# Block B's q and k: x tiles 2 and 3 by Strassen's algorithm, alternating with plain groups, with the loads around them at other times

## The chip, the cores and the metric

The kernel runs on one core of a Trainium2 chip. Its engines work side by side, each through a list of instructions of its own: TensorE (PE) multiplies matrices, with PEld its loads of weights; VectorE (DVE) and ScalarE (ACT) do elementwise work; GpSimd (POOL) does elementwise work too; SyncE (SP) issues the transfers, which 16 DMA engines carry out. SBUF is the memory on the chip, PSUM the eight banks that matmuls write to. The metric is the device time of one execution in microseconds, lower is better, as a median of several.

## The reference

Two attention blocks over the same shapes, S = 2048 rows, D = 640, 32 heads of 20. Both begin with x @ wqkv and end with a product by wo; the outputs are concatenated.

```python
# both blocks
q, k, v = split((x @ wqkv).reshape(1, 2048, 3, 32, 20))   # x 2048x640, wqkv 640x1920
# A: every position s looks at s, s-2, ... s-14 (W = 8, dilation 2), earlier ones masked
kg, vg = k[:, :, s - 2 * arange(8)], v[:, :, s - 2 * arange(8)]
out_A = softmax(einsum("bhsd,bhswd->bhsw", q, kg) * 20 ** -0.5) weighted over vg, then @ wo
# B: full attention
out_B = softmax(q @ k.T * 20 ** -0.5) @ v, then @ wo
```

## The kernel before, in words

Each factor of a product of x and a weight is split into a high part, rounded to a shorter format (fp32r), and the low rest; a product of 128x128 by 128x512 is then three matmuls (PASSES: high-high, high-low, low-high). x is transposed in DRAM and cut into four tiles of 512 columns for each block; D = 640 is five chunks of 128 rows, of which a tile keeps four in a buffer of the tag "big" (xn) and the fifth in "last0" or "last1" (xl). `a_split(hi, lo, raw)` makes a split: ScalarE casts the high part, VectorE subtracts for the low one.

The program runs through stages on TensorE:

- A's q and k, until 137.3 us. `a_four` computes them already by the Strassen-Winograd scheme (sums of quarters of x and of w instead of an eighth product), and `a_narrow` the remaining narrow columns. POOL makes the x sums for it (`x_sums`).
- B's q and k, 137.3 to 274.2 us, the stage that the change is about. The 1280 columns of q and k are ten groups of 128 (the order is MS), taken two at a time: for each pair, four x tiles by two groups, 40 results of 128x512 with 15 matmuls each. A result goes from its PSUM bank by a ScalarE cast (high part) and a VectorE subtraction (low part) to an SBUF tile (tags "pa" and "pb", three buffers each), and from there by one SP transfer to DRAM, as `kb_d` or `qb_d`. A weight group comes by one transfer into a "stg" buffer and is split into a "w" buffer (four of these).
- V of both blocks, from 274.2 us. Blocks 0 and 1 of the loop are four plain groups of 15 matmuls 128x128x320 each; their results (`ro`, tag "r", four buffers) are copied by ScalarE and stored to `va_d`. From block 2 the matmuls are made of 64-row halves, and between them stand the first products of B's q and k (`b_max`, which finds the maxima of the softmax), from tiles `bk` and `bq` that `b_pieces(0)` loads back from `kb_d` and `qb_d`. bk and bq take buffers of the tag "big".
- the main loop, where B's scores and values alternate on TensorE, and at the end the products by wo.

A's attention itself runs on POOL all along, in units paced by `a_pace` with constants such as QK_US; twelve units (the scores of three row tiles) stand ahead of V.

The order of instructions on each engine is fixed by the program: the wrapper `InOrder` keeps it as written, `tick()` counts steps, and `after(n, fn)` puts code n steps later. So an instruction that waits holds everything behind it on its engine. SP issues almost all transfers in one such order. The tags' numbers of buffers set when a load can start: a tile gets the buffer of the oldest one of its tag when that has been read for the last time. PSUM banks are handed out by `all_banks` in a fixed turn of eight in the stages before V; in V, a list `free` of four is used.

In the listing, all operations that go through the wrapper carry its line, L71; groups in the profile are told apart by the names of the tiles and their shapes.

Of the kernel before, what the change touches and what calls it, by code (L numbers as in the profile page):

```python
# [17 lines left out]
S = 2048  # L18
# [32 lines left out]
QK_US = 3.42  # L51
# [24 lines left out]
def attention_pair(ctx, tc, xa, wqk_a, wv_a, wo_a, xb, wqk_b, wv_b, wo_b, oa, ob):  # L76
# [498 lines left out]
    XB, WB = [], []  # L575
# [88 lines left out]
    def w_ask(n):  # L664
        w, fns = m_pieces(MS[n])
        WB.append(w)
        fns[0]()
# [20 lines left out]
    p_next[:] = "bbbaaa"  # L688
    b_load(1)
    a_narrow(2)  # L690
    b_load(2)
# [7 lines left out]
    XB.append(w)  # L699


# [33 lines left out]
    def x_raw(c):  # L735

        out = []
        for a, b in PAIRS:
            raw = p_tile()[:, :(b - a) * 512].rearrange("p (k c) -> p k c", c=512)
            sp.dma_start(raw, (xa, xb)[c // 4][a * 128:b * 128, c % 4 * 512:c % 4 * 512 + 512].rearrange("(k p) c -> p k c", p=128))  # L740
            out.append((a, b, raw))
# [4 lines left out]
    def xv_ask():  # L746

        t = columns(0)
        XV.append((t, None))
        for j, (tag, bufs) in enumerate((("vb", 2), ("aot", 1))):  # L750
            raw = sb.tile([128, 1280], F32, tag=tag, bufs=bufs, name="xr")
            for k, c0, n, r in ((2 * j, 0, 2, raw[:, :1024].rearrange("p (k c) -> p k c", c=512)), (4, 256 * j, 1, raw[:, 1024:].unsqueeze(1))):
                c = r.shape[2]
                sp.dma_start(r, xa[k * 128:(k + n) * 128, c0:c0 + c].rearrange("(k p) c -> p k c", p=128))
                u, m = t[k // (KC - 1)], k % (KC - 1)
                after(8, a_split, u[:, 0, m:m + n, c0:c0 + c], u[:, 1, m:m + n, c0:c0 + c], r)

    groups = 0
    gp.us = 0.0
    for m in range(0, 10, 2):  # L760
        nxt = []
        for n in range(4):
            for j in range(2):
                p = next(banks)
                for k in range(KC):
                    for i, (wi, xi) in enumerate(PASSES):
                        pe.matmul(p, WB[j][:, wi, k], chunk(XB[n], xi, k), start=(k == 0 and i == 0),
                                  stop=(k == KC - 1 and i == 2))
                c = MS[m + j]
                o = (0, 1) if c < KC else (1, 0)  # L770
                pt = p_pair(F32R)
                act.copy(pt[:, o[0]], p)
                dve.tensor_tensor(pt[:, o[1]], p, pt[:, o[0]].bitcast(F32), ALU.subtract)
                after(1, sp.dma_start, dst_b(c, n).rearrange("t p c -> p t c"), pt.bitcast(F32))
                tick()
                if loads:
                    loads.pop(0)()
                if m < 8 and n == (m == 0):
                    w, loads = m_pieces(MS[m + 2 + len(nxt)])
                    nxt.append(w)  # L780
                elif m == 6 and (n, j) == (2, 0):
                    xv_ask()
                elif m == 6 and (n, j) == (3, 0):
                    w0, loads = wide_pieces(wv_a[0])
                elif m == 8:
                    g8 = 2 * n + j
                    if g8 == 1:
                        k_loads, q_loads = b_pieces(0)
                    elif 1 < g8 < 6:
                        k_loads.pop(0)()  # L790
                        if g8 == 5:
                            xraw = x_raw(1)
                        if g8 == 3:
                            wait[0] = 7
                            w1, more = wide_pieces(wv_a[1])
                            for fn in more:
                                fn()
                    elif g8 == 6:
                        for _ in range(4):
                            q_loads.pop(0)()  # L800
                groups += 1
                if groups > 4:
                    a_pace(A_SLOW * QK_US * groups)
        WB = nxt
# [472 lines left out]
    def x_parts(c, raws, second=gp):  # L1277
# [6 lines left out]
        for a, b, raw in raws:  # L1284
            u, m = t[a // (KC - 1)], a % (KC - 1)
            hi, lo = (u[:, x, m:m + b - a] for x in range(2))
            act.copy(hi, raw)
            if c not in (2, 3):
                second.tensor_tensor(lo, raw, hi.bitcast(F32), ALU.subtract)

# [7 lines left out]
    for block in range(15):  # L1298
        c, half = divmod(block, 2)
        s0 = c % 4 * 4  # L1300
        if block < 2:
            for s in range(s0, s0 + 4):
                v_group(c, half, s)
                v_tick(2.2, False)
                if (block, s) == (0, 3):
                    x_parts(1, xraw, dve)
                    xraw = x_raw(2)
# [227 lines left out]
```

## Time and profile before

| | |
|---|---|
| median of 3 runs | 1720.01 us (1719.5 to 1721.14) |
| the profiled execution | 1720.44 us, of which the span on the core is 1718.4 |
| TensorE busy | 1708.8 us, 99% of the span |
| VectorE, ScalarE, POOL busy | 1458.6, 1335.6, 1316.5 us |
| B's q and k on TensorE | 137.29 to 274.21 us |
| V's blocks 0 and 1 on TensorE | 274.21 to 291.90 us |

How to read the rows: a row of a window gives the stretch, its length, then busy time and number of instructions of each engine, TensorE's granted clock (1.00 is full speed), the mean busy share of the 16 DMA engines and GB/s. A row of a group gives line, engine, operation, output tile <- input tiles, shapes and number, then busy time and mean ns of one, then the idle time ahead of it and what ended it. A row of the timeline gives start and duration in us, engine, line, operation, tiles and number of instructions run together; in brackets the idle time before it with what ended it. A row of waits gives the engine, what it waited for, then us in total, number of waits and the longest. SPq is the queue of transfers that SP issues.

### The profile page before, as it was taken

How to read it: one execution, taken by the hardware profiler on the slowest of the kernel's cores; microseconds unless marked ns; L12 is line 12 of the kernel's file. 1: busy time of each engine (PE TensorE's matmuls, PEld its weight loads, DVE VectorE, ACT ScalarE, POOL GpSimd, SP SyncE). 2: the span in 40 equal slices, each digit the busy share in tenths (PEclk: the TensorE clock that was granted, in tenths of full speed). 3: DMA queues.
4: the chain of work that ended last, by engine and by line, in shares of the span. 5: the costliest groups of instructions: out<-in, count | busy, mean ns of one | idle time of the engine just before them, and what ended most of it. 6: DMA issues, size and time to landing. Idle time of an engine off the chain costs nothing.

```text
span 1718.4 us, 34879 instructions
## 1 busy us (share of the span) xinstructions
PE 1708.8 (99%) x12627; PEld 990.3 (58%) x12627; DVE 1458.6 (85%) x1975; ACT 1335.6 (78%) x2637; POOL 1316.5 (77%) x1175
## 2 busy tenths in 40 slices
PE   9999999999999999999999999999999999999999
PEld 8888889999544544444444444444444445434459
DVE  8554334889899999999999999999999999999537
ACT  6213224232799999999999999999999999999972
POOL 4110990589999999999999999999999973486352
PEclk9999999999999999999999999999999999999999
DMA  6548979966843364345436345542644532111123
GB/s 196 183 158 265 327 259 281 304 196 207 221 138 104 102 185 132 102 128 161 129 112 168 115 124 129 171 136 84 164 135 117 140 99 75 40 49 41 34 73 118
DMA packets 207844, 253.53 MB, mean 148 GB/s; under 512 B 89788, under 2 KB 131004, under 8 KB 206680
## 3 DMA queue, kind: packets, MB, share of 16 engines
q1 hardware_dynamic: 206232, 249.67, 48.8%
q8 instruction: 99, 1.62, 0.4%
q10 hardware_dynamic: 1440, 1.64, 0.3%
q14 instruction: 73, 0.60, 0.1%
HBM read 183.70 MB, written 67.53 MB: 146 GB/s over the span
## 4 chain that ended last, share of the span: by engine, by line
PE 82%; POOL 9%; DVE 3%; ACT 2%; DMA 2%; issue 1%; SPq 0%; POOLq 0%; DVEq 0%; ACTq 0%
PE ps_st L71 82%; POOL akv L71 5%; DVE mx L71 3%; ACT stg L71 1%; POOL braw L71 1%; POOL ao L71 1%; POOL xn L71 1%; POOL ww L71 0%; DMA stg<-wqk_a 0%; DMA stg<-xa 0%; DVE wg L71 0%; POOL al L71 0%; SPq L71 0%; DMA stg<-wo_a 0%; ACT more L71 0%
## 5 line engine op out<-in xcount | busy, mean ns | idle before, releaser
L71 DVE TENSOR_REDUCE mx<-ps_st 128x1 f32<-128x512 f32 (+1 forms) x1504 | 1228.6, 876 | 56.1 <-PE ps_st L71 46.7
L71 ACT ACTIVATE stg<-ps_st 128x512 f32<-128x512 f32 x2000 | 1046.1, 630 | 41.4 <-PE ps_st L71 28.0
L71 PE MATMUL ps_st<-bk,bq 60*128 60x512 f32 x2048 | 553.7, 436 | 0.7 <-DVE mx L71 0.3
L71 PE MATMUL ps_st<-bq,bk 62*128 62x512 f32 x2048 | 549.0, 432 | 1.0 <-ACT e L71 0.9
L71 PE MATMUL ps_st<-stg,vb 128*32 128x512 f32 x4000 | 531.6, 604 | 0.4
L71 PEld LDWEIGHTS ps_st<-bq,bk 62*128 62x128 f32 x2048 | 274.9, 184 | 399.2 <-ACT stg L71 241.8
L71 POOL TENSOR_TENSOR braw<-braw,more 128x512 f32<-128x512 f32 x224 | 289.4, 1292 | 58.8 <-ACT more L71 56.6
L71 PEld LDWEIGHTS ps_st<-bk,bq 60*128 60x128 f32 x2048 | 257.1, 184 | 108.2 <-DVE mx L71 61.3
L71 POOL TENSOR_TENSOR akv<-akv 128x640 f32<-128x640 f32 (+3 forms) x304 | 284.0, 934 | 14.4
L71 POOL TENSOR_TENSOR akv<-akv,aq 128x1280 f32<-128x1280 f32 x64 | 188.2, 2941 | 76.5 <-PE ps_st L71 76.5
L71 PEld LDWEIGHTS ps_st<-stg,vb 128*32 128x32 f32 x4000 | 79.5, 108 | 143.5 <-issue 70.4
L71 POOL TENSOR_TENSOR akv<-akv,al 128x1280 f32<-128x1280 f32 x64 | 151.5, 2367 | 0.7 <-DMA akv<-va_d 0.5
L71 ACT COPY more<-ps_st 128x512 f32<-128x512 f32 x224 | 137.6, 614 | 2.7 <-PE ps_st L71 2.2
L71 ACT COPY ro<-ps_st 128x320 f32<-128x320 f32 (+2 forms) x130 | 52.6, 453 | 108.7 <-PE ps_st L71 76.9
L71 DVE TENSOR_TENSOR ro<-ps_st,ro 128x320 f32<-128x320 f32 (+1 forms) x112 | 61.9, 574 | 86.2 <-PE ps_st L71 78.2
L71 PE MATMUL ps_st<-ww,xn 64*128 64x320 f32 (+1 forms) x1392 | 123.9, 307 | 0.0
L71 PEld LDWEIGHTS ps_st<-ww,xn 64*128 64x128 f32 (+1 forms) x1392 | 117.7, 185 | 3.6 <-ACT stg L71 0.7
L71 PE MATMUL ps_st<-xn,w 128*128 128x512 f32 x480 | 115.9, 390 | 0.0
L71 PE MATMUL ps_st<-ww,aot 64*128 64x320 f32 x960 | 100.4, 309 | 1.5 <-POOL aot L71 1.5
L71 PEld LDWEIGHTS ps_st<-xn,w 128*128 128x128 f32 x480 | 90.0, 188 | 19.5 <-DVE xn L71 0.2
L71 PEld LDWEIGHTS ps_st<-ww,aot 64*128 64x128 f32 x960 | 90.4, 186 | 8.0 <-POOL aot L71 2.0
L71 ACT CAST stg<-ps_st 128x512 fp32r<-128x512 f32 x40 | 23.4, 589 | 76.1 <-PE ps_st L71 76.1
(116 smaller groups left out, 1329.4 us busy)
## 6 DMA issues: line engine op xcount, KB each, us to landing
akv<-ka_d SPq DMA_DIRECT2D x128, 320.0 KB
akv<-va_d SPq DMA_DIRECT2D x128, 320.0 KB
kb_d<-stg SPq DMA_DIRECT2D x20, 512.0 KB
qb_d<-stg SPq DMA_DIRECT2D x20, 512.0 KB
bk<-kb_d SPq DMA_DIRECT2D x16, 640.0 KB
bq<-qb_d SPq DMA_DIRECT2D x64, 160.0 KB
stg<-xb SPq DMA_DIRECT2D x16, 512.0 KB
rb<-s_d SPq DMA_DIRECT2D x128, 64.0 KB
```

The source lines that it names most:

```text
L71: return self.tc.keep_in_program_order(op(*a, **k))
```

## The change

The 600 matmuls of B's q and k become 570. x tiles 0 and 1 stay plain (`b_plain`). For each pair of weight groups, x tiles 2 and 3 become four Strassen parts (`b_four`: one, second, third, fourth, with 12, 15, 15 and 12 matmuls) which take sums of quarters of the weights (`s_sums` on VectorE, split by `s_parts` into the tiles sx) and of x (four differences on POOL in `other`, split into the tiles tx, named T1 to T4, by `t_split`, with VectorE's subtraction for T2 and T3 and POOL's for T1 and T4). Products are added from PSUM into the result tiles by VectorE (`plus`), ScalarE casts the high part (`high`), VectorE subtracts in SBUF (`done`). The list `plan` sets the order: five plain groups, then a Strassen part and a plain group in turn; the last pair's four Strassen parts follow each other.

Loads and other work move with it. x tiles 2 and 3 come raw into "akv" buffers, as do V's x tiles 0 and 1 (`xv_ask`, before in "vb" and "aot", or in the p tiles). `b_load` of x tiles 0 and 1 is at steps 17 and 20 of A's stage. The weights of V are asked for at two parts of the plan (`v_ask`), and `b_pieces(0)` is called after the last part. The memsets of four tiles with ones go from VectorE to POOL behind the stage, QK_US is 3.25 for 3.42, and the list of PSUM banks is turned by two at V's block 9.

On SP, from the last results of q and k to V's stores (qb_d<-stg is a result's store, bk and bq are loads for b_max, stg<-wv_a and stg<-xa are loads for V, va_d<-ro is a V store). Before:

```order
L71 DMA bk<-kb_d 40x4096
L71 DMA qb_d<-stg 128x2x512
L71 DMA bk<-kb_d 22x4096
L71 DMA stg<-xa 128x2x512 x2
L71 DMA stg<-xa 128x512
L71 DMA qb_d<-stg 128x2x512
L71 DMA bq<-qb_d 20x1024
L71 DMA bq<-qb_d 40x1024
L71 DMA bq<-qb_d 20x1024
L71 DMA bq<-qb_d 40x1024
L71 DMA qb_d<-stg 128x2x512
L71 DMA va_d<-ro 128x320 x4
```

After the change:

```order
L71 DMA bk<-kb_d 40x4096
L71 DMA bk<-kb_d 22x4096
L71 DMA bk<-kb_d 40x4096
L71 DMA bk<-kb_d 22x4096
L71 DMA va_d<-ro 128x320 x2
L71 DMA bq<-qb_d 20x1024
L71 DMA bq<-qb_d 40x1024
L71 DMA va_d<-ro 128x320
L71 DMA bq<-qb_d 20x1024
L71 DMA bq<-qb_d 40x1024
L71 DMA va_d<-ro 128x320
```

All four bk loads now stand in one piece behind the last q stores, and the V stores behind them.

On VectorE, at the start of B's q and k (stg<-ps_st is a result, ve a tile of ones, w a weight's low part, xn and xl those of x, sx and tx the low parts of sums; the raw halves of x tiles 2 and 3 are xr). Before:

```order
L71 TENSOR_TENSOR xn<-stg,xn 128x1024 x2
L71 TENSOR_TENSOR xl<-stg,xl 128x512
L71 MEMSET ve 128x347 x4
L71 TENSOR_TENSOR stg<-ps_st,stg 128x512 x3
L71 TENSOR_TENSOR xn<-stg,xn 128x1024
L71 TENSOR_TENSOR stg<-ps_st,stg 128x512
L71 TENSOR_TENSOR xn<-stg,xn 128x1024
```

After the change:

```order
L71 TENSOR_TENSOR xn<-xr,xn 128x1024
L71 TENSOR_TENSOR xl<-xr,xl 128x256
L71 TENSOR_TENSOR w<-stg,w 128x640
L71 TENSOR_TENSOR stg<-ps_st,stg 128x512
L71 TENSOR_TENSOR xn<-xr,xn 128x1024
L71 TENSOR_TENSOR sx<-stg,sx 128x256
L71 TENSOR_TENSOR tx<-stg,tx 128x256 x2
L71 TENSOR_TENSOR sx<-stg,sx 128x256
L71 TENSOR_TENSOR stg<-ps_st,stg 128x512
L71 TENSOR_TENSOR xl<-xr,xl 128x256 x2
L71 TENSOR_TENSOR stg<-ps_st,stg 128x512
L71 TENSOR_TENSOR w<-stg,w 128x640
```

The second pair's first weight (w) and the parts of the weights' sums (sx, and tx for two of them) now stand there, between the first results; the tiles of ones are gone from it.

The diff, cut to what the text speaks of:

```diff
 NEG = -1.0e30
 STEP = 2.36
 AHEAD = 2.4
-QK_US = 3.42
+QK_US = 3.25
 V_US = 2.72
 A_SLOW = 0.78
...
+    def w_raw(m, j):
+        WR[m, j] = sb.tile([128, KC, 128], F32, tag="stg", bufs=3, name="stg")
+        sp.dma_start(WR[m, j], wqk_b[MS[2 * m + j]])
+    def w_take(m, j):
+        w = WT[m, j] = sb.tile([128, 2, KC, 128], F32R, tag="w", bufs=4, name="w")
+        a_split(w[:, 0], w[:, 1], WR[m, j])
+    SB, TB = {}, {}
...
+    def x_pair():
+        t2, t3 = columns(2), columns(3)
+        XB[2], XB[3] = t2, t3
+        r2 = akv_raw(xb, 2)
+        after(2, other, t2, t3, r2)
+    def other(t2, t3, r2):
+        r3 = akv_raw(xb, 3)
+        (x11, x21), (x12, x22) = ((r[0][3], r[2][3]) for r in (r2, r3))
...
+        def t_split(n, raw, eng):
+            hi, lo = TB[n]
+            for k in range(2):
+                act.copy(hi[k], raw[:, k])
+                eng.tensor_tensor(lo[k], raw[:, k], hi[k].bitcast(F32), ALU.subtract)
+        for p in r2:
+            after(3, put, t2, p)
+        after(7, put, t3, r3[2])
+        for out, a, b in ((x11, x12, x11), (x12, x22, x12), (x22, x22, x11), (x21, x21, x22)):
+            after(7, pool, out, a, b, ALU.subtract)
+        after(5, w_take, 1, 0)
+        after(6, homes)
+        after(7, s_parts, 0)
+        for p in (r3[1], r3[3]):
+            after(8, put, t3, p)
+        after(9, w_take, 1, 1)
+        for n, (at, raw, eng) in {2: (9, x22, dve), 3: (9, x12, dve), 1: (10, x11, gp), 4: (10, x21, gp)}.items():
+            after(at, t_split, n, raw, eng)
+        after(8, w_raw, 1, 1)
+    def s_sums(m):
+        (a11, a12), (a21, a22) = ((WR[m, j][:, :2], WR[m, j][:, 2:4]) for j in range(2))
+        for out, a, b, op in ((a22, a21, a22, ALU.add), (a21, a11, a21, ALU.subtract), (a11, a22, a11, ALU.subtract), (a12, a12, a11, ALU.subtract)):
+            dve.tensor_tensor(out, a, b, op)
+    def s_parts(m):
+        j0, j1 = (WR.pop((m, j)) for j in range(2))
+        for n, r in (("2", j0[:, :2]), ("3", j1[:, :2]), ("1", j1[:, 2:4]), ("4", j0[:, 2:4])):
+            a_split(*(u.rearrange("p (k c) -> p k c", c=128) for u in SB[n]), r)
...
     for at, *fns in ((2, lambda: x_load(2)), (4, lambda: x_split(2, xr[2])), (5, lambda: x_sums(xr[2])), (7, lambda: s_split(2, xr[2]), constants),
                      (9, lambda: x_load(3)), (11, lambda: x_split(3, xr[3])), (12, lambda: x_sums(xr[3])), (14, lambda: s_split(3, xr[3])),
-                     (20, lambda: b_load(0))):
+                     (17, lambda: b_load(0)), (20, lambda: wait.__setitem__(0, 6), lambda: b_load(1))):
         steps_a[at] = fns
     for n in (1, 2, 3):
         for r in range(2):
             a_four(n, r, step)
         if n == 1:
             a_narrow(1)
-    wait[0] = 3
-    w_ask(0)
-    w_ask(1)
+    for j in range(2):
+        w_raw(0, j)
+        after(3, w_take, 0, j)
+    after(4, s_sums, 0)
     p_next[:] = "bbbaaa"
-    b_load(1)
+    x_pair()
+    after(4, w_raw, 1, 0)
...
-    ones = [sb.tile([128, 16 * VC + 11], F32, tag=tag, bufs=3 if tag == "raw" else 2, name="ve")
-            for tag in ("raw", "rb", "raw", "rb")]
-    for t in ones:
-        dve.memset(t, 1.0)
-    w, loads = x_pieces(xb, 3)
-    XB.append(w)
...
+        def prod(a, b, c4=None):
+            p = next(banks)
...
+        def tile_of(j, n):
+            pt = P4[j, n] = p_pair(F32R)
+            return low(j, n)
+        def low(j, n):
+            return P4[j, n][:, 1 if MS[m + j] < KC else 0].bitcast(F32)
+        def plus(p, a, out):
+            dve.tensor_tensor(out, p, a, ALU.add)
+        def high(j, n):
+            act.copy(P4[j, n][:, 0 if MS[m + j] < KC else 1], low(j, n))
+        def done(j, n):
+            pt, o = P4[j, n], MS[m + j] >= KC
+            dve.tensor_tensor(pt[:, 1 - o], low(j, n), pt[:, 0 + o].bitcast(F32), ALU.subtract)
+            b_out(MS[m + j], n, pt)
+        def one():
+            act.copy(tile_of(0, 2), prod("11", "11"))
+            p = prod("S2", "T2")
+            plus(p, low(0, 2), tile_of(0, 3))
+        def second():
+            plus(prod("12", "21", (0, 2)), low(0, 2), low(0, 2))
+            high(0, 2)
+            p = prod("S3", "T3")
+            plus(p, low(0, 3), tile_of(1, 2))
+            done(0, 2)
+        def third():
+            p = prod("S1", "T1")
+            plus(p, low(0, 3), low(0, 3))
+            plus(p, low(1, 2), tile_of(1, 3))
+            plus(prod("S4", "22", (0, 3)), low(0, 3), low(0, 3))
+            high(0, 3)
+            done(0, 3)
+        def fourth():
+            plus(prod("22", "T4", (1, 2)), low(1, 2), low(1, 2))
+            high(1, 2)
+            plus(prod(None, None, (1, 3)), low(1, 3), low(1, 3))
+            done(1, 2)
+            high(1, 3)
+            done(1, 3)
+        return [one, second, third, fourth]
...
+    plain = [(0, 0, 0), (0, 0, 1), (1, 0, 0), (0, 1, 0), (0, 1, 1)]
+    rest = iter([(m, n, j) for m in range(5) for n in range(2) for j in range(2) if (m, n, j) not in plain])
+    plan = [("p", *u) for u in plain]
+    for m in range(5):
+        for n in range(4):
+            plan.append(("q", m, n))
+            if m < 4:
+                plan += [("p", *u) for u in islice(rest, 1)]
...
+        def one(hi, lo, raw):
+            act.copy(hi, raw)
+            gp.tensor_tensor(lo, raw, hi.bitcast(F32), ALU.subtract)
+        for i, p in enumerate(akv_raw(xa, n)):
+            after(*((3 + i, put, t, p) if n else (3, put, t, p, one)))
+    def v_ask():
+        w = wide_pieces(wv_a[len(w01)])
+        w01.append(w[0])
+        for fn in w[1]:
+            fn()
+    def pieces():
+        loads_0.extend(b_pieces(0))
+        for n, fn in enumerate(loads_0[0] + loads_0[1][:4]):
+            after(n // 2 + 1 + n // 4, fn)
...
+    def at(what, fn, *args):
+        events.setdefault(what, []).append((fn, args))
+    for m in range(4):
+        at(("q", m, 0), s_sums, m + 1)
+        if m < 3:
+            at(("q", m, 0), w_raw, m + 2, 0)
+            at(("q", m, 2), w_take, m + 2, 0)
+        at(("q", m, 2), s_parts, m + 1)
+        if m < 3:
+            at(("q", m, 2), w_raw, m + 2, 1)
+            at(("q", m, 3), w_take, m + 2, 1)
+    at(("q", 3, 2), wait.__setitem__, 0, 2)
+    at(("q", 3, 2), v_ask)
+    at(("p", 4, 1, 0), xv_ask, 0)
+    at(("q", 4, 1), wait.__setitem__, 0, 3)
+    at(("q", 4, 1), v_ask)
+    at(("q", 4, 2), xv_ask, 1)
+    at(("q", 4, 3), pieces)
     gp.us = 0.0
-    for m in range(0, 10, 2):
-        nxt = []
-        for n in range(4):
-            for j in range(2):
-                p = next(banks)
-                for k in range(KC):
-                    for i, (wi, xi) in enumerate(PASSES):
...
-        WB = nxt
+    four = []
+    for n, what in enumerate(plan):
+        if what[0] == "p":
+            b_plain(*what[1:])
+        else:
+            if what[2] == 0:
+                four = b_four(what[1])
+            four[what[2]]()
+        tick()
+        for fn, args in events.pop(what, ()):
+            fn(*args)
+        if n > 5:
+            a_pace(A_SLOW * QK_US * (n + 1))
+    assert not events and next(rest, None) is None
+    (w0, w1), (k_loads, q_loads) = w01, loads_0
+    q_loads = q_loads[4:]
+    ones = [sb.tile([128, 16 * VC + 11], F32, tag=tag, bufs=3 if tag == "raw" else 2, name="ve")
+            for tag in ("raw", "rb", "raw", "rb")]
+    for t in ones:
+        gp.memset(t, 1.0)
...
     for block in range(15):
+        if block == 9:
+            free.extend([free.pop(0), free.pop(0)])
         c, half = divmod(block, 2)
         s0 = c % 4 * 4
         if block < 2:
```

More of the change, by code (lines that the diff above doesn't have):

```diff
@@ new lines, in b_plain @@
+    def b_plain(m, n, j):
+        c, W = MS[2 * m + j], WT[m, j]
+        p = next(banks)
+        for k in range(KC):
+            for i, (wi, xi) in enumerate(PASSES):
+                pe.matmul(p, W[:, wi, k], chunk(XB[n], xi, k), start=(k == 0 and i == 0), stop=(k == KC - 1 and i == 2))
+        o = (0, 1) if c < KC else (1, 0)
+        pt = p_pair(F32R)
+        act.copy(pt[:, o[0]], p)
+        dve.tensor_tensor(pt[:, o[1]], p, pt[:, o[0]].bitcast(F32), ALU.subtract)
+        b_out(c, n, pt)
```

116 lines of the change are left out of this document (57 added, 59 removed).

## The prediction

> **What bounds the kernel now.** I read the page's busy times first, then TensorE's waits, then the stretches of the program, then the groups of instructions and the queues of the stretch that changes.
>
> ```profile
> span 1718.4 us, 34879 instructions
> PE 1708.8 (99%) x12627; PEld 990.3 (58%) x12627; DVE 1458.6 (85%) x1975; ACT 1335.6 (78%) x2637; POOL 1316.5 (77%) x1175
> ```
> ```profile
> PE ps_st L71 <- POOL aot L71: 1.5, 2, 0.8
> ```
> ```profile
> 137.30:274.20 136.90, 136.90 (x602) 112.52 (x601) 51.03 (x67) 37.92 (x63) 84.11 (x80) 1.00 0.85 285
> 274.20:291.90 17.70, 17.70 (x122) 17.50 (x120) 5.71 (x7) 7.13 (x13) 0.00 (x0) 1.00 0.89 273
> ```
> TensorE is busy for 1708.8 of 1718.4 us; the largest sum in the list of its waits is 1.5 us. In block B's q and k (137.30 to 274.20) and the first two blocks of V (to 291.90) it never pauses, and its clock is 1.00 in both (the column ahead of the DMA share). So time goes only if matmuls go, and any wait that the change opens on TensorE is paid in full. In the same rows VectorE (51.03) and ScalarE (37.92) have much room in q and k; the DMA engines have little, at shares of 0.85 and 0.89.
>
> ```profile
> 137.29 2.93 PE L71 MATMUL ps_st<-xn,w 128*128 128x512 f32 x12
> ...
> 144.14 2.88 PE L71 MATMUL ps_st<-xn,w 128*128 128x512 f32 x12
> ```
> ```profile
> 274.21 1.92 PE L71 MATMUL ps_st<-ww,xn 128*128 128x320 f32 x12
> ...
> 291.90 2.10 PE L71 MATMUL ps_st<-ww,xn 64*128 64x320 f32 x23
> ```
> **Matmuls removed.** The first row is the start of q and k, the third the start of V. Forty groups of 15 are 600 matmuls in 274.21 - 137.29 = 136.92 us, 0.2282 us each. A pair of weight groups on x tiles 2 and 3 takes 12 + 15 + 15 + 12 = 54 instead of 60, all of the same size, so five pairs lose 30: -6.85 us. V would start at 267.36, and its block 2 at 291.90 - 6.85 = 285.05. A pair now holds 114 matmuls, 26.0 us.
>
> **VectorE.**
>
> ```profile
> L71 DVE TENSOR_TENSOR stg<-ps_st,stg 128x512 fp32r<-128x512 f32 x39 | 26.7, 688 | 59.1 <-ACT stg L71 59.1
> L71 ACT CAST stg<-ps_st 128x512 fp32r<-128x512 f32 x39 | 22.9, 589 | 73.3 <-PE ps_st L71 73.3
> L71 DVE TENSOR_TENSOR w<-stg,w 128x640 fp32r<-128x640 f32 x8 | 10.9, 1360 | 8.4 <-ACT w L71 8.4
> L71 DVE TENSOR_TENSOR xn<-xr,xn 128x1024 fp32r<-128x1024 f32 x2 | 2.4, 1222 | 0.3 <-ACT xn L71 0.3
> L71 DVE TENSOR_TENSOR xl<-xr,xl 128x256 fp32r<-128x256 f32 x2 | 0.8, 418 | 0.0
> L71 ACT CAST xn<-xr 128x1024 fp32r<-128x1024 f32 x2 | 2.1, 1052 | 0.0
> L71 ACT CAST xl<-xr 128x256 fp32r<-128x256 f32 x2 | 0.8, 401 | 0.0
> L71 ACT CAST w<-stg 128x640 fp32r<-128x640 f32 x8 | 5.8, 731 | 9.6 <-DMA stg<-wqk_b 9.6
> ```
> Per pair VectorE has 4 plain results and 8 sums from PSUM (12 x 0.688), 4 differences in SBUF (`done`, 128x512 again and taken at the same 0.688), 4 weight sums and 4 parts (8 x 0.418) and 2 weight splits (0.83): 8.26 + 2.75 + 3.34 + 1.66 = 16.0 us, against TensorE's 26.0. ScalarE gets one more 0.589 us cast a pair, hidden in its idle 99 of 137 us. The 14 operations that read two SBUF tiles are the doubtful ones:
>
> ```profile
> 162.34 0.83 DVE L71 TENSOR_TENSOR w<-stg,w 128x640 fp32r<-128x640 f32 x1 [1.22 <-ACT w L71]
> ...
> 234.56 2.63 DVE L71 TENSOR_TENSOR w<-stg,w 128x640 fp32r<-128x640 f32 x1
> ```
> ```profile
> 21.44 6.08 POOL L71 TENSOR_TENSOR rw<-rw 128x1024 f32<-128x1024 f32 x2 [0.69 <-DVE wc L71]
> ...
> 168.47 2.94 POOL L71 TENSOR_TENSOR akv<-akv,aq 128x1280 f32<-128x1280 f32 x1 [76.45 <-PE ps_st L71]
> ...
> 233.54 2.96 POOL L71 TENSOR_TENSOR akv<-akv,aq 128x1280 f32<-128x1280 f32 x1
> ...
> 305.62 0.74 POOL L71 TENSOR_TENSOR al<-al,am 128x256 f32<-128x256 f32 x1 [48.09 <-DVE am L71]
> ```
> ```profile
> L71 POOL TENSOR_TENSOR akv<-akv 128x640 f32<-128x640 f32 (+3 forms) x48 | 42.0, 875 | 3.8
> ```
> The weight split is 0.83 us ahead of POOL's first unit (168.47). At 234.56 it takes 2.63 and ends at 237.19, 0.69 us after POOL's multiply (233.54 + 2.96 = 236.50): it stood behind the rest of a whole POOL instruction. Of the eight in the 1360 ns row two ran ahead of POOL's start, so the other six averaged (8 x 1.360 - 2 x 0.83)/6 = 1.54, a wait of 0.71 each. At that rate 14 operations make 16.0 + 9.9 = 25.9 us a pair: just TensorE's pace. I take no loss in the steady state. [...]
>
> **The start of the stage.** The hand-written order puts this on TensorE's path. x tile 2's halves go into a buffer that A's last group frees at 137.29. ScalarE then casts two pieces of 1.05 and two of 0.40, copies two results of A (0.43 for the copy further below, which is a little larger) and casts the second pair's first weights (0.73): 4.4 us, about 141.8, and VectorE's 0.83 for the low part ends at 142.6; the third plain group needs it from 144.14 on. T2 is needed by the first pair's second product, after five plain groups and six matmuls (137.29 + 81 x 0.2282 = 155.8), and by the same rows is ready at about 153.3. So the chains have some 1.5 and 2.4 us of room if VectorE is not held up. But POOL now makes the four x sums of 128x1024 just then (two of that size took 6.08, 3.04 each), and VectorE's queue holds five operations with two SBUF inputs up to that weight split and ten more up to T2. Lower bound: they slip past, 0. Upper bound: a sum ahead of nearly every one puts the split at 147.4 (2.8 us late) and, behind it, the load and cast of the pair's other weights (its buffer is released by VectorE's parts) and T2 another 2.5: 5.3. I take the excess of the 1360 ns row over 0.83, 0.53 an operation, which is the nearest mean: four after the first make 2.1, 0.6 beyond the room; eight more make 4.2, less 2.4 and the 0.6 already paid, 1.2. Together +1.8.
>
> **The start of V.** b_pieces(0) moves behind the last Strassen part, since bk and bq take the buffers of x tiles 2 and 3. SP's order has the four bk loads after the last q stores and ahead of all V stores.
>
> ```profile
> 269.73 0.43 SPq L71 DMA_DIRECT2D bk<-kb_d  x1
> ```
> ```profile
> 437.17 1.44 SPq L71 DMA_DIRECT2D bk<-kb_d  x4
> ...
> 445.16 0.33 SPq L71 DMA_DIRECT2D stg<-wo_a  x1
> ...
> 454.79 0.80 SPq L71 DMA_DIRECT2D akv<-va_d  x2
> ```
> ```profile
> SPq L71 <- DMA bk<-kb_d: 12.9, 4, 4.4
> ```
> ```profile
> bk<-kb_d SPq DMA_DIRECT2D x16, 640.0 KB
> ```
> ```profile
> 290.72 0.43 ACT L71 COPY ro<-ps_st 128x320 f32<-128x320 f32 x1 [4.39 <-DMA va_d<-ro]
> 291.64 1.18 ACT L71 COPY ro<-ps_st 128x320 f32<-128x320 f32 x3 [0.49 <-PE ps_st L71]
> ```
> Before, the last bk went out at 269.73, 4.5 us ahead of V's start. Even so the fifth V copy stood 4.39 us for the first V store (the "r" tag has four buffers) and started at 290.72, when block 2 (291.90) needed the banks of copies five and six within 1.2 us. The same four loads issued in one go at 437.17 held SP, by 12.9 us in four waits, until 454.79: 17.6 us. In the changed order V's start is 267.36, the last q stores' differences end about 2.5 us later, and the loads go out at about 270.8; the last lands at about 288.4, the first V store behind it about 288.7, copies five and six end by 289.2 and 289.8, and TensorE waits from 285.05 to some 289.9. That is +4.9. Bounds: 0, if the loads ran at the 273 GB/s of the stretch (four of at most the 640 KB of the issue list, 9.6 us, landed by 280.4); upwards 6.6, if the last q stores or the second V store add 1.7. I take 4.9, since the row at 437.17 shows the very same four loads. bq comes behind them, at about 290 to 291; its first use is a few matmuls into block 2, which by then has just begun.
>
> **The rest, at nothing.** The memsets of `ones` and the low parts of V's first x tile, on POOL, lie in its 48.09 us wait for the softmax's maximum (up to 305.62); without it they would push A's units back by their own length (a sum of 128x1024 is 3.04). SP's x loads are four DMAs instead of three for x tiles 2 and 3 and V's tile 1, issued ahead of need while SP has idle time. A's pace (3.25 for 3.42) follows the shorter stage. The turn of the bank list at block 9 changes which bank, not when. V's weights are asked for at the parts q32 and q41, several groups of 3.4 us ahead of V's start.
>
> **Sum** on the profiled execution, 1720.44 us (1718.4 of span and 2.04 around it): -6.85 + 1.8 + 4.9 = -0.15. That execution lies 0.43 over the median 1720.01; against the median the sum is 1719.9, which I give as 1720.0.
>
> **Rivals.**
> 1. The covers hold: V stores pass the bk loads, or the loads take nearer 9.6 than 17.6 us. For it: 273 GB/s is the stretch's mean. Against: the four waits of SP on them. Then 1713.2 without early wait, 1715.0 with 1.8.
> 2. Slower: VectorE, taking turns with POOL, becomes the bound of q and k. Room is (26.0 - 16.0)/14 = 0.715 an operation, and the mean of six was 0.71. Each 0.06 more over the four pairs in which POOL works is 14 x 0.06 x 4 = 3.4 us of lag at the stage's end, which PSUM's eight banks hide from TensorE there but which makes the last q stores, hence bk and the V stores, that much later. From 0.775 on it decides: 1723.5; at 0.80 it is 14 x 0.085 x 4 = 4.8, 1724.8. The early chain's 5.3 instead of 1.8 has the same cause and alone gives 1723.5. For it: the 2.63 us at 234.56; and a unit of POOL is one multiply of 2.96 and four additions of 0.875, back to back, so that an operation which comes at any moment and stands until the running instruction ends waits on average (2.96 x 2.96/2 + 4 x 0.875 x 0.875/2)/6.46 = 0.9 us, 16.0 + 12.6 = 28.6 us a pair and 4 x 2.6 = 10.4 us of lag: 1730. Against: the measured mean of six, and POOL starts late in the first pair.
> 3. The pause lowers TensorE's clock. No row of before has a TensorE pause of this length inside the kernel, and all its clocks are 1.00, so nothing shown speaks for or against. If one V group (2.2 us, an eighth of 274.21 to 291.90) ran at half rate after the pause, that is 2.2: 1722.2. [...]
>
> That the matmuls are not saved is excluded by the order, which has 54 in a pair.
>
> **How the numbers follow.** A measurement can tell about 0.2% (3.44 us) from no change: faster is below 1716.6, slower above 1723.4. Main case, early wait 0 to 2.8 and V's start 4.9: 1718.1 to 1720.9, chance 0.42. Rival 1, 1713.2 to 1716.4: 0.28. Rival 2, 1723.5 to 1730: 0.20. Rival 3, 1720 to 1723: 0.10. Thus faster 0.28, same 0.51, slower 0.21. The range 1713.5 to 1724.5 leaves out about 0.06 of rival 1 and 0.12 of rival 2.
>
> **What would show it.** Right: V's first group at 267 to 270; TensorE idle 4 to 6 us at the start of block 2, with ScalarE's fifth copy waiting for va_d and SP waiting for bk; small TensorE waits near 144 and 156 for VectorE's w and tx; w splits of 0.8 to 2.6 us. Wrong: no pause at block 2 (rival 1); V's first group past 272 or VectorE busy without idle time in q and k (rival 2); a clock under 1.00 after the pause (rival 3).

## The result, and the profile after

The changed kernel takes 1738.4 us (median of 4 runs, 1738.0 to 1739.5) against 1720.0 of the kernel before on the same chip (median of 3 runs): a ratio of 1.0107, 95% interval 1.0087 to 1.0127. A fourth run of the kernel before took 2237.4 us and is left out. The change makes the kernel slower by some 18 us, although its q and k have 30 matmuls less. The profiled execution has a span of 1736.3 us, 17.9 more than before.

TensorE's waits, first those of the whole kernel after the change, then its timeline where they stand (start, duration, matmuls; in brackets the idle time ahead):

```profile
PE ps_st L71 <- ACT ro L71: 8.6, 1, 8.6
PE ps_st L71 <- DVE w L71: 7.2, 2, 4.2
```
```profile
136.68 2.93 PE L71 MATMUL ps_st<-xn,w 128*128 128x512 f32 x12
...
187.73 4.14 PE L71 MATMUL ps_st<-xn,w 128*128 128x512 f32 x10 [4.21 <-DVE w L71]
191.71 0.85 PE L71 MATMUL ps_st<-xl,w 128*128 128x512 f32 x3
...
215.93 0.73 PE L71 MATMUL ps_st<-xn,w 128*128 128x512 f32 x2 [0.78 <-ACT w L71]
219.70 4.63 PE L71 MATMUL ps_st<-xn,w 128*128 128x512 f32 x10 [3.03 <-DVE w L71]
224.13 1.48 PE L71 MATMUL ps_st<-xl,w 128*128 128x512 f32 x3
...
280.53 1.92 PE L71 MATMUL ps_st<-ww,xn 128*128 128x320 f32 x12
...
306.89 3.97 PE L71 MATMUL ps_st<-ww,xn 64*128 64x320 f32 x24 [8.61 <-ACT ro L71]
```
The stage begins 0.6 us earlier than before (136.68 for 137.29) and ends 6.3 later (280.53 for 274.21). It contains three waits, 8.0 us together, all for a weight's split (4.21, 0.78 and 3.03), and behind two of them the matmuls are slow: the ten at 187.73 take 3.98 us to the next group, where ten at 0.2282 are 2.28. The same reckoning over the rows behind 219.70 gives 2.9 us more, so the two pauses cost 4.6 beside themselves. -6.85 - 0.61 + 8.0 + 4.6 is 5.1; the remaining 1.2 lie mostly in the last matmuls ahead of the pauses (two take 0.73 us there, where two at 0.2282 are 0.46). The 0.61 is scatter and no gain of the change: in bk_late (below), which is the kernel before up to there, the stage starts at 136.80. Block 2 of V then stands 8.6 us for its banks, and its first 24 matmuls take 3.97, where the first 23 took 2.10 before, another 1.9. With 6.3 these make 16.8 of the 17.9.

The windows show the clock (column ahead of the DMA share) fall in those places and stay at 1.00 between them:

```profile
187.70:191.70 4.00, 3.97 (x10) 3.12 (x11) 1.59 (x3) 0.00 (x0) 3.77 (x5) 0.57 1.01 338
191.70:215.00 23.30, 23.30 (x103) 18.96 (x101) 22.33 (x23) 5.83 (x12) 22.05 (x20) 1.00 0.45 152
219.70:226.90 7.20, 7.20 (x19) 5.72 (x20) 7.10 (x6) 0.59 (x1) 6.89 (x7) 0.58 1.02 342
226.90:267.00 40.10, 40.10 (x177) 32.81 (x176) 29.10 (x42) 11.85 (x24) 15.71 (x16) 1.00 0.70 238
306.80:311.10 4.30, 4.21 (x29) 4.09 (x31) 0.00 (x0) 1.29 (x4) 0.00 (x0) 0.51 0.89 249
```
Why the weights are late stands in two views of VectorE by form and stretch. From 166 to 244 us POOL works on A without a break:

```profile
L71 DVE TENSOR_TENSOR stg<-stg 128x512 fp32r<-128x512 f32 x9 | 16.7, 1869 | 2.3 <-ACT stg L71 2.1
L71 DVE TENSOR_TENSOR stg<-ps_st,stg 128x512 f32<-128x512 f32 x19 | 12.4, 681 | 4.4 <-DMA kb_d<-stg 2.4 <-PE ps_st L71 2.0
L71 DVE TENSOR_TENSOR stg<-stg 128x256 f32<-128x256 f32 x8 | 11.5, 1435 | 0.2
L71 DVE TENSOR_TENSOR w<-stg,w 128x640 fp32r<-128x640 f32 x5 | 7.8, 1566 | 0.0
L71 DVE TENSOR_TENSOR sx<-stg,sx 128x256 fp32r<-128x256 f32 x6 | 7.8, 1301 | 0.0
```
From 244 to 270 us POOL stands idle, and the same instructions read:

```profile
L71 DVE TENSOR_TENSOR stg<-ps_st,stg 128x512 f32<-128x512 f32 x10 | 6.6, 684 | 1.5 <-PE ps_st L71 1.5
L71 DVE TENSOR_TENSOR stg<-stg 128x512 fp32r<-128x512 f32 x6 | 4.1, 692 | 0.9 <-ACT stg L71 0.7
L71 DVE TENSOR_TENSOR stg<-stg 128x256 f32<-128x256 f32 x4 | 1.7, 423 | 0.1
L71 DVE TENSOR_TENSOR sx<-stg,sx 128x256 fp32r<-128x256 f32 x2 | 0.8, 418 | 0.0
L71 DVE TENSOR_TENSOR w<-stg,w 128x640 fp32r<-128x640 f32 x1 | 0.8, 826 | 0.6 <-ACT w L71 0.6
```
A `done` in SBUF is 1869 ns beside a working POOL and 692 without; a weight sum 1435 and 423; a part 1301 and 418; a weight split 1566 and 826. A sum that takes one input from PSUM is 681 and 684: it doesn't notice POOL. So it is not the load on VectorE in general, but two SBUF inputs. At 182 to 188 us VectorE's queue holds two `done` and behind them the split for which TensorE stands:

```profile
181.54 4.06 DVE L71 TENSOR_TENSOR stg<-stg 128x512 fp32r<-128x512 f32 x2
185.53 2.15 DVE L71 TENSOR_TENSOR w<-stg,w 128x640 fp32r<-128x640 f32 x1
```
They take 6.2 us; at 0.69 and 0.83 they would take 2.2. At V's start the loads' queue and ScalarE's row:

```profile
288.75 2.40 SPq L71 DMA_DIRECT2D bk<-kb_d  x4
291.25 0.85 SPq L71 DMA_DIRECT2D va_d<-ro  x2
```
```profile
306.41 0.83 ACT L71 COPY ro<-ps_st 128x320 f32<-128x320 f32 x2 [14.18 <-DMA va_d<-ro]
```
The four bk loads go out 8.2 us after V's start, and the copies five and six stand until 306.41, 17.7 us after the first bk. In the last third of that time the DMA engines (share in the column ahead of GB/s) are far from full:

```profile
299.60:304.00 4.40, 0.00 (x0) 0.00 (x0) 0.00 (x0) 0.00 (x0) 0.40 (x2) 0.63 0.61 150
304.00:306.40 2.40, 0.00 (x0) 0.00 (x0) 0.00 (x0) 0.00 (x0) 0.00 (x0) 0.50 0.56 212
```

### The profile page after: what moved, and what is told of

It reads as the page before. It is cut to its first block, busy times and chain, and to the rows that moved or that the text cites. A ratio compares the mean times of both kernels' runs of the same rounds, so it can differ in the third digit from the quotient of the medians.

```text
span 1736.3 us, 34989 instructions
## 1 busy us (share of the span) xinstructions
PE 1711.1 (99%) x12597; PEld 989.9 (57%) x12597; DVE 1539.4 (89%) x2053; ACT 1345.3 (77%) x2672; POOL 1347.4 (78%) x1191
## 4 chain that ended last, share of the span: by engine, by line
PE 82%; POOL 5%; DVE 5%; DMA 5%; issue 1%; ACT 1%; SPq 1%; POOLq 0%; DVEq 0%; ACTq 0%
PE ps_st L71 82%; DVE mx L71 3%; POOL akv L71 2%; DMA stg<-wo_a 1%; DMA va_d<-ro 1%; ACT stg L71 1%; POOL braw L71 1%; SPq L71 1%; DVE stg L71 1%; DMA bk<-kb_d 1%; POOL ww L71 0%; POOL ao L71 0%; POOL xn L71 0%; DVE tx L71 0%; DMA stg<-xb 0%
## 5 line engine op out<-in xcount | busy, mean ns | idle before, releaser
L71 POOL TENSOR_TENSOR akv<-akv 128x640 f32<-128x640 f32 (+3 forms) x304 | 288.3, 948 | 14.4
L71 PE MATMUL ps_st<-xn,w 128*128 128x512 f32 x300 | 77.9, 407 | 8.2 <-DVE w L71 7.2
L71 POOL TENSOR_TENSOR ao<-ao,akv 128x640 f32<-128x640 f32 x48 | 75.0, 1562 | 2.0
L71 PEld LDWEIGHTS ps_st<-xn,w 128*128 128x128 f32 x300 | 58.5, 197 | 22.8 <-DVE w L71 8.4
```

Of the source, the lines that this page charges most:

```text
L71: return self.tc.keep_in_program_order(op(*a, **k))
```

## The experiments

Theory 1: instructions of VectorE with two SBUF inputs stand behind POOL's, so that the weights' splits (and with them TensorE) and the last q stores (and with them bk and V's stores) are late; the long pauses also slow the clock (to 0.57, 0.58 and 0.51 behind 4.21, 3.03 and 8.61 us). Rivals: the moved loads and SP's order alone; the mere number and chain of VectorE's instructions. All ratios are to the kernel before in the same series.

**plain40: the loads without the algorithm.**

```diff
-                four = b_four(what[1])
+                four = [lambda m=what[1], n=n, j=j: b_plain(m, n, j) for n in (2, 3) for j in range(2)]
...
-        after(7, s_parts, 0)
...
-            after(at, t_split, n, raw, eng)
...
-        at(("q", m, 0), s_sums, m + 1)
```
x tile 3 is split whole instead, and all sums for the algorithm are left out.

> The changed kernel without Strassen's algorithm: x tiles 2 and 3 are multiplied plainly (600 matmuls again), without sums of x and of weights, with the changed loads, the changed order of groups and the late bk loads. Theory 1 (VectorE, whose instructions with two SBUF inputs stand behind POOL's, is late in q and k because of the Strassen parts' extra ones): no wait for a weight in q and k, stage 137 us, the bk loads go out about 3 us after V's start instead of 8.2, block 2 waits about 5 instead of 8.6 and the clock costs 2 to 3 more: about 1727. Rival (the moved loads and the order of SP alone make the waits, whatever VectorE has to do): waits of 7 to 8 us in q and k stay and the time is about 1743, since 30 matmuls come back.

1727.6 us, ratio 1.0044 (1.0028 to 1.0061). No wait in q and k; the one of block 2 remains:

```profile
273.81 1.92 PE L71 MATMUL ps_st<-ww,xn 128*128 128x320 f32 x12
...
297.40 3.97 PE L71 MATMUL ps_st<-ww,xn 64*128 64x320 f32 x24 [5.83 <-ACT ro L71]
```
As theory 1 expected; the bk loads go out 2.9 us after V's start. So the change without the algorithm costs 7.6 us, and the Strassen parts, which save 6.85 in matmuls, add 11 to that instead.

**bk_late: the bk loads, with the first four bq loads behind them, moved in the kernel before.**

```diff
                     elif 1 < g8 < 6:
-                        k_loads.pop(0)()
...
-                    elif g8 == 6:
-                        for _ in range(4):
-                            q_loads.pop(0)()
+                    elif g8 == 7:
+                        for i, fn in enumerate(k_loads + q_loads[:4]):
+                            after(i // 2 + 1 + i // 4, fn)
+                        q_loads = q_loads[4:]
```


> The kernel before, with one part of the change alone: the four bk loads and the first four bq loads wait until the last group of q and k, and so stand in one piece ahead of the V stores. Nothing else differs. If V stores stand behind the bk loads, block 2 waits about 5 us and the clock costs 2 to 3 more: 1727. If that wait needs VectorE's late results as well, it is hidden here: 1720.

1724.2 us, ratio 1.0026 (1.0017 to 1.0036): +4.5 by the ratio. The wait is shorter than expected, 2.33 us, the slow matmuls behind it nearly as dear (24 in 3.87 us, for 3.97 in the changed kernel):

```profile
294.41 3.87 PE L71 MATMUL ps_st<-ww,xn 64*128 64x320 f32 x24 [2.33 <-ACT ro L71]
```

**pool_late: POOL kept out of part of the stage.**

```diff
-        if n > 5:
+        if n > 16:
             a_pace(A_SLOW * QK_US * (n + 1))
```


> The changed kernel with POOL's first units of A let in only from the 17th entry of the plan on (instead of the 7th), so that POOL reads nothing in SBUF between its x work (to 161 us) and about 195 to 200; fewer units are then done ahead of V. VectorE's and TensorE's lists in q and k are the same. Theory 1 (two-input instructions stand behind POOL's): ahead of POOL's start VectorE's differences in SBUF (done) take 0.69 and the parts 0.42, the wait of 4.2 us near 183 is gone; the second wait (near 212) stays at some 3 us. Rival (the chain of loads, casts and sums makes the waits): both stay. The total is less telling, as A's units come later: 1730 to 1740.

1741.6 us, ratio 1.0118 (1.0101 to 1.0135). POOL's first unit starts at 207.27. Ahead of it (here 162 to 198 us) VectorE's differences are at their bare length, and no wait stands in TensorE's list; behind it both return, a pair later than in the changed kernel:

```profile
L71 DVE TENSOR_TENSOR stg<-stg 128x512 fp32r<-128x512 f32 x6 | 4.1, 691 | 1.5 <-ACT stg L71 1.4
L71 DVE TENSOR_TENSOR w<-stg,w 128x640 fp32r<-128x640 f32 x2 | 1.6, 824 | 0.0
```
```profile
207.27 2.95 POOL L71 TENSOR_TENSOR akv<-akv,aq 128x1280 f32<-128x1280 f32 x1 [45.54 <-DMA akv<-ka_d]
```
```profile
229.66 2.57 PE L71 MATMUL ps_st<-xn,w 128*128 128x512 f32 x10 [0.33 <-DVE w L71]
239.61 1.22 PE L71 MATMUL ps_st<-xn,w 128*128 128x512 f32 x2 [3.95 <-ACT w L71]
244.19 4.61 PE L71 MATMUL ps_st<-xn,w 128*128 128x512 f32 x10 [3.36 <-DVE w L71]
```
The wait of 4.2 us near 183 is gone, and so is the next one, since POOL began even later than I meant. TensorE's and VectorE's lists are those of the changed kernel, so the chain of loads, casts and sums alone makes no wait. That decides for theory 1. The total is worse: SP, whose list holds the loads for POOL's units, stands 8.2 us for POOL from 280 to 316 us, the bk loads go out 13.9 us after V's start (278.19), and block 2 waits 14.6 us.

**psum: fewer differences with two SBUF inputs.**

```diff
+        def last(p, j, n):
+            FIN[j, n] = p
+            plus(p, low(j, n), p)
...
-            dve.tensor_tensor(pt[:, 1 - o], low(j, n), pt[:, 0 + o].bitcast(F32), ALU.subtract)
+            dve.tensor_tensor(pt[:, 1 - o], FIN[j, n], pt[:, 0 + o].bitcast(F32), ALU.subtract)
```
ScalarE's cast of such a result (`high`) reads the bank too.

> The changed kernel with one edit: a Strassen result's last sum is written back to its PSUM bank, so that the subtraction for the low part (done) reads PSUM and SBUF instead of two SBUF tiles. The number of instructions on each engine is the same. Theory 1 (instructions with two SBUF inputs stand behind POOL's): the 16 or so of these, 1.2 us in the mean while POOL works, take 0.7, the waits for the weights' splits shrink from 4.2 and 3.8 to some 1.5 each, and with the clock the time falls by 5 to 10: 1728 to 1733. Rival (VectorE is late because of the number and the chain of its instructions): no change, 1738.

1724.7 us, ratio 1.0029 (1.0018 to 1.0039): 13 us less than the changed kernel, more than expected. The 20 sums into PSUM take 689 ns, no more than into SBUF. One wait in q and k is left, 0.95 us, with the ten matmuls behind it at full speed (2.56 us), and V starts at 268.39. Block 2 still waits:

```profile
L71 DVE TENSOR_TENSOR ps_st<-ps_st,stg 128x512 f32<-128x512 f32 x20 | 13.4, 689 | 3.0 <-PE ps_st L71 3.0
```
```profile
210.46 2.56 PE L71 MATMUL ps_st<-xn,w 128*128 128x512 f32 x10 [0.95 <-DVE w L71]
268.39 1.92 PE L71 MATMUL ps_st<-ww,xn 128*128 128x320 f32 x12
...
295.22 3.62 PE L71 MATMUL ps_st<-ww,xn 64*128 64x320 f32 x24 [9.07 <-ACT ro L71]
```

**w_later, bk_early, both: each wait moved away by order.**

```diff
-    rest = iter([(m, n, j) for m in range(5) for n in range(2) for j in range(2) if (m, n, j) not in plain])
+    rest = iter([(m, n, j) for m in range(5) for j in range(2) for n in range(2) if (m, n, j) not in plain])
...
-    at(("q", 4, 3), pieces)
+    at(("q", 4, 0), pieces)
```
The first edit is w_later, the second bk_early, and both has the two. bk_early also keeps the first bq loads three steps longer, so that these go out as in the changed kernel.

> The changed kernel with the plain groups of a pair in another order: first the pair's first weight group on both x tiles, then the second, so that the second weight group's split is needed one plain group and one Strassen part (some 6 us) later. If VectorE is only late for a moment there (a matter of latency), the waits of 4.2 and 3.8 us and the slow clock behind them (4.6) go: about 1726. If VectorE is slower than TensorE throughout, the time comes back at the next product or as later q stores and a longer wait at block 2: 1733 to 1738.

1729.1 us, ratio 1.0054 (1.0039 to 1.0069). The waits for weights shrink from 8.0 to 2.1 us and V starts at 269.95:

```profile
PE ps_st L71 <- ACT w L71: 1.2, 1, 1.2
PE ps_st L71 <- DVE w L71: 0.9, 2, 0.6
```
```profile
218.00:244.00 26.00, 24.52 (x107) 19.46 (x105) 25.04 (x24) 7.62 (x16) 24.75 (x21) 1.00 0.61 208
```
```profile
269.95 1.92 PE L71 MATMUL ps_st<-ww,xn 128*128 128x320 f32 x12
```
So most of the loss in the stage was a matter of when the split is due. That VectorE has room is not shown: from 218 to 244 us it is busy for 25.0 of 26 us (9.2 in the kernel before), and the waits that are left all stand there or just behind. The wait at block 2 stays at 8.8.

> The changed kernel with the buffers of bk and bq asked for three parts earlier, so that bk takes x tile 1's buffer and its four loads go out during the last pair, as before the change. Theory (V stores stand behind the bk loads in the queues): the wait of 8.6 us at block 2 and the slow clock behind it (about 3) go, 1727. Rival (the loads then hold up others, or V's x tile 1, whose low parts VectorE ends only at 299, is what comes next): a wait of 1 to 5 us stays at block 2, 1729 to 1735.

1734.5 us, ratio 1.0081 (1.0066 to 1.0096): 4 to 5 us less than the changed kernel. The rival was right: of the wait at block 2 5.7 us stay, now in block 1.

> The changed kernel with both edits: the other order of plain groups and the early bk loads. If the two waits are independent and were all of the loss, 1738.4 - 12.6 - 11.6 = 1714. If VectorE is slower than TensorE throughout, what the first edit saves comes back at V's start: 1722 or more.

1729.0 us, ratio 1.0060 (1.0041 to 1.0078): the second edit adds nothing to the first, where 1714 was expected if the waits were independent. In "both" the wait left block 2 and came up in block 1:

```profile
290.91 3.57 PE L71 MATMUL ps_st<-ww,xn 128*128 128x320 f32 x12 [8.10 <-ACT ro L71]
```
```profile
289.48 1.04 ACT L71 CAST xn<-xr 128x1024 fp32r<-128x1024 f32 x1 [9.20 <-DMA xr<-xa]
```
The loads of V's x tile 1, now behind bk, land late, and ScalarE waits for them with V's copies queued behind; bk_early has the same wait (7.21).

**warm: is it the pause that slows the matmuls?**

```diff
+        if (m, n, j) in ((2, 0, 1), (3, 0, 1)):
+            for _ in range(12):
+                pe.matmul(p, WT[m, 0][:, 0, 0], chunk(XB[0], 0, 0), start=True, stop=True)
```


> The changed kernel with 12 further matmuls ahead of each of the two plain groups that wait for a weight's split; they write the group's own bank, which it overwrites, and so fill about 2.7 us of the waits. If a pause of over some 3 us lowers the clock, the rest (1.5 us) does not, and the 13 matmuls behind each wait run at 0.23 us instead of up to 0.44: 4 us less, 1734. If the slow matmuls behind the pauses have another cause, no change: 1738.

1737.5 us, ratio 1.0101 (1.0086 to 1.0116): not distinguishable from the changed kernel by the total. The two pauses, however, separate the cases:

```profile
187.80 4.15 PE L71 MATMUL ps_st<-xn,w 128*128 128x512 f32 x10 [2.10 <-DVE w L71]
...
219.83 2.60 PE L71 MATMUL ps_st<-xn,w 128*128 128x512 f32 x10 [1.39 <-DVE w L71]
```
Behind 1.39 us idle the ten matmuls are at full speed (2.60 us, for 4.63 in the changed kernel behind 3.03), behind 2.10 us they are still slow (4.15). The pause is the cause; the expected bound of 3 us for it was too high, so only one of the two was cured, and a new wait of 1.15 us for a weight's cast came up later.

**v2, v3, v4, v7: towards a version that keeps the gain.** v2 has w_later's order, psum's sums, bk loads from the last pair's first part on, and x tile 1's splits behind V's fourth group:

```diff
-            after(n // 2 + 1 + n // 4, fn)
+            after(n // 2 + 1 if n < 4 else n // 2 + 6, fn)
...
-    at(("q", 4, 3), pieces)
+    at(("q", 3, 3), pieces)
...
-            after(*((3 + i, put, t, p) if n else (3, put, t, p, one)))
+            after(*((6, put, t, p) if n else (3, put, t, p, one)))
```


> The changed kernel with the plain groups in the other order, the last sums in PSUM, the bk loads already at the last pair's first two Strassen parts, and the splits of V's x tile 1 only behind V's fourth group (with the early bk loads alone they stood ahead of V's copies on ScalarE and moved the wait to block 1). If the losses are the weights' splits and the traffic at V's start, nearly all of the 30 matmuls is kept: 1715 to 1719. If V's x tile 1 lands late behind the bk loads, block 2 waits 3 to 5 us for it: 1720 to 1725.

1717.7 us, ratio 0.9988 (0.9979 to 0.9998): 2 us less than the kernel before and 20 less than the changed one. q and k run without a wait and V starts at 267.03, 7.2 us earlier than before; 5.2 of these are lost again in block 1, in two waits and slow matmuls, so that block 2 starts at 289.93:

```profile
267.03 1.92 PE L71 MATMUL ps_st<-ww,xn 128*128 128x320 f32 x12
...
278.82 1.43 PE L71 MATMUL ps_st<-ww,xn 128*128 128x320 f32 x8 [2.84 <-ACT ro L71]
280.80 1.43 PE L71 MATMUL ps_st<-ww,xn 128*128 128x320 f32 x4 [0.55 <-DVE ww L71]
```
Here the eight matmuls behind 2.84 us are still at full speed (1.43 us, 0.18 each; 12 take 1.92 at 267.03), and only the four behind the next wait of 0.55 us are slow (1.43 us, 0.36 each); the mean clock is 1.00 from 226 to 280 us and 0.94 from 280 to 310. In warm the ten matmuls directly behind 2.10 us are slow: the clock does not fall at the same moment behind every pause.

v3 has the low parts of V's x tile 0 on VectorE; v4, on top, the bk loads behind the second half of V's weights.

> The version with four edits (other order of plain groups, last sums in PSUM, early bk loads, later splits of x tile 1), and the low parts of V's x tile 0 on VectorE instead of POOL. SP stood 9.1 us there for the raw buffers of tile 0, which POOL's low parts hold. If these block the loads of x tile 1 and the last q stores, they go out some 5 us earlier and 1 to 3 us are gained: 1715. If the late halves of V's weights (ScalarE waited 5 us for them) are what counts, no change: 1717.7.

1719.5 us, ratio 0.9991 (0.9982 to 1.0001): no gain over v2.

> The version v3 with the four bk loads behind the second half of V's weights instead of ahead of it. If ScalarE's wait for these weights (it holds V's copies behind it, 2.8 us on TensorE) comes from the bk loads ahead of them, it goes and 2 to 4 us are gained over v3: 1712 to 1714. If the V stores then stand behind bk again, a wait of 2 to 5 us comes back at block 2: 1716 to 1719.

1722.4 us, ratio 1.0016 (1.0006 to 1.0025). The wait in block 1 goes, and one of 6.1 us comes back at block 2. v7 is v2 with eight buffers for V's first results, the bk loads half ahead of, half behind the second half of V's weights, and the splits of x tile 1 two steps later.

> The version v2 with the second pair of bk loads behind the second half of V's weights, eight buffers instead of four for V's first results (so that no copy waits for a V store), and the splits of x tile 1 two steps later. If the V stores are what holds block 2, it starts without a wait and the time is 1712 to 1714. If all that V needs comes through the same full queues, the wait only changes its name (x tile 1 in place of the stores), 2 to 4 us of it stay, and the time is 1715 to 1718.

1720.0 us, ratio 1.0000 (0.9991 to 1.0008). The wait changed its name, as in the second case of the expectation, and the time lies 2 us over what that gave. No copy waits for a store any more; block 2 starts at 284.52 without a wait, stands 1.1 us for x tile 1 and then 3.3 for bq:

```profile
291.01 0.76 PE L71 MATMUL ps_st<-bk,bq 60*128 60x512 f32 x1 [2.16 <-DMA bq<-qb_d]
292.90 1.19 PE L71 MATMUL ps_st<-bk,bq 60*128 60x512 f32 x3 [1.13 <-DMA bq<-qb_d]
```
The four versions move one wait between V's weights, its stores, its x tile 1 and bq. All of these go through the 16 DMA engines, which in v2, v4 and v7 are busy for 0.86 to 0.99 of the time from 267 to 310 us; which of the transfers could be made cheaper was not tried.

## Why the prediction was wrong

The forecast was 1720.0, range 1713.5 to 1724.5; measured 1738.4, beyond every rival's figure too. In the terms of the sum, -6.85 + 1.8 + 4.9 became -6.85 + 0 + 10.5, and a term that stood at nothing, VectorE's lag inside the stage, became 13.8 (8.0 + 4.6 + 1.2).

- **Matmuls removed, -6.85.** Right. In v2, with no wait in the stage, it lasts from 136.93 to 267.03, 130.10 us, where 570 matmuls of 0.2282 make 130.07.
- **VectorE's steady state, 0.** This is the step that failed, in its cost and in its wait. I took the mean of six weight splits, a wait of 0.71 us, for all 14 operations, found 25.9 us a pair against TensorE's 26.0, and called it even. By the two views of VectorE above, the four groups waited in the mean 1.18 (done), 1.01 (sums), 0.74 (w) and 0.88 (parts) us; with these the 14 operations make 16.0 + 13.8 = 29.8 us a pair, more than TensorE's 26.0. And the length of the pair was the wrong thing to compare with. TensorE does not need a pair's work by the end of the pair: it needs one instruction, the second weight group's split, at a set time, and two `done` stand ahead of it in the queue. Rival 2 named the cause and gave a lag of 10.4 us and 1730, but let PSUM's banks hide the lag inside the stage; in the trace TensorE waits there three times for a weight and never for a bank. Rival 2's wait of 0.9, from the lengths of POOL's instructions, was nearer to the measured mean (13.8/14, 0.99) than 0.71. Either mend alone takes away most of the loss: psum, which shortens the waits and keeps the order, brings V's start from 280.53 to 268.39, w_later, which moves the split, to 269.95. Which of the two errors weighs more stays open. Left out of the sum besides, without a cost that shows: ScalarE's casts of the four parts, 1.5 us a pair.
- **The start of the stage, +1.8.** Wrong the other way: 0. The step was that x tile 2's buffer comes free only with A's last group at 137.29. ScalarE began the cast at 131.80, while A's last groups still ran:

```profile
131.80 1.05 ACT L71 CAST xn<-xr 128x1024 fp32r<-128x1024 f32 x1
```
- **The start of V, +4.9.** The mechanism was right and the four bk loads' time too (17.7 us from 288.75 to the copies' release at 306.41, against 17.6 to the end of SP's waits; 17.6 again in bk_late, some 20 in psum and plain40). What makes it so long was not tried; the two rows above with shares of 0.61 and 0.56 speak against a lack of DMA engines as such. By itself, in bk_late, it costs 4.5. Mis-sized was the moment at which they go out: 8.2 us after V's start and not 3.4; so the wait was 8.6, over the upper bound of 6.6. SP, which takes its list in order, stood from 265 to 310 us 9.4 us for VectorE's results and 6.0 for its splits of V's weights. The late Strassen results are not all of it: in psum the bk loads still go out 6.2 us after V's start.
- **Rival 3, the clock,** was given 2.2 us once and a chance of 0.10. The half rate in it was an estimate; the windows behind the pauses show clocks of 0.57, 0.58 and 0.51. It happened behind all three long pauses (4.21, 3.03 and 8.61 us), 1.7, 2.9 and 1.9 us: 6.5 together. The length of the pause alone does not fix the moment: 2.10 (warm) and 2.33 us idle (bk_late) were enough, 1.39 (warm) was not, and behind 2.84 in v2 eight matmuls (1.43 us) still ran at full speed.
- **The rest, at nothing.** Not quite: the low parts of V's x tile 0 on POOL stand beside VectorE's splits of V's weights (three took 4.83 us at 272.83 in the changed kernel). They were no part of the sum. v3, which is v2 with this edit, moved them to VectorE and gained nothing, so their share stays open.

## What to carry to other kernels

Before more work goes to an engine with idle time, look in the trace how long its instructions take while another engine works, by the number of their inputs in SBUF: here a VectorE difference of two SBUF inputs took 1869 ns beside a working POOL and 692 without, a sum with one input from PSUM 681 and 684. A busy share of 37% (VectorE's in q and k before) says little when instructions become that much longer. Compare an in-order queue not with the length of the stage but with the moment at which the next engine needs one certain instruction of it, and put what is waited for ahead of what is not. Where PSUM can hold the intermediate, letting one input stay there took 13 us off without a single instruction less.

## What the runs showed of the hardware that was not expected

- Where TensorE paused for 2.10 us or more in q and k and in V's first blocks, slow matmuls followed (in warm ten of 128x512 in 4.15 us behind 2.10, instead of 2.60 behind 1.39; clocks of 0.57, 0.58 and 0.51 in the changed kernel behind 4.21, 3.03 and 8.61), behind 1.39 in warm none. Behind 2.84 us in v2 eight matmuls ran at full speed first (1.43 us), so the moment of the fall is not fixed by the pause alone; what fixes it is not shown. The pause of 2.10 us in warm thus cost nearly twice its length (1.55 more in ten matmuls), that of 2.33 in bk_late too (24 matmuls in 3.87, where 23 took 2.10 before).
- VectorE's sum of PSUM and SBUF written back to PSUM takes 689 ns for 128x512 (psum), as long as one written to SBUF (681 in the changed kernel).
- Beside a POOL that never rests, a VectorE instruction of 0.42 us with two SBUF inputs took 1.3 to 1.4 in the mean (1301 and 1435 ns for 418 and 423 without POOL, in the changed kernel), three times its length. The wait in it, 0.9 to 1.0 us, is no shorter than that in one of 0.83 us (0.74); POOL's instructions there take 0.3 to 3.5.
